# Holding six chunk loads for a last read on VectorE, and dealing the mixer's steps unevenly

## The chip, the cores and the metric

The kernel runs on one core of a Trainium2 chip. It uses TensorE (PE), VectorE (DVE), ScalarE (ACT), GpSimd (POOL), and SyncE (SP), which issues every DMA of this kernel. The metric is device time in microseconds. The kernel before took 374.99 us, the median of three runs (372.95, 374.99 and 376.47).

## The reference

Two blocks follow one another. The first is a linear attention with a decaying state, for 4 batches, 8 heads, 768 tokens and a head width of 48:

```python
for t in range(S):
    kt, vt, rt = (k[:, :, t], v[:, :, t], r[:, :, t])
    cur = np.einsum('bhd,bhe->bhde', u[None] * kt, vt)
    y[:, :, t] = np.einsum('bhd,bhde->bhe', rt, state + cur)
    state = w[None, :, :, None] * state + np.einsum('bhd,bhe->bhde', kt, vt)
```

Its heads side by side are `x` (4 x 768 x 384), which goes into the second block, a gated mixer:

```python
h = np.maximum(x @ w_in, 0.0)                 # d_ff = 1024
u, v = (h[..., :512], h[..., 512:])
v_n = (v - mean(v)) / np.sqrt(var(v) + 1e-06) # over the 512 of a token
v_s = np.einsum('ts,bsd->btd', w_spatial, v_n) + b_spatial[None, :, None]
out = (u * v_s) @ w_out
```

All of it is float32.

## The kernel before

The attention is cut into 24 chunks of 128 tokens, six to each batch. The main loop (L605) has one **period** for each chunk, numbered from 0, and one before them, -1. A period `i` goes through these parts, and each engine does its share of them in the order in which they are written; nothing is reordered.

- `g2(i)` (L362): TensorE finishes chunk `i`. It reads `r` out of the tile `rk` (L379), and then `v` out of the tile `rkv` (L389). It is 112 matmuls as the profile counts them, 88 for the first chunk of a batch.
- `fin(i)` (L391): ScalarE copies the result to `xh` (L399). Up to chunk 6 TensorE then makes the low part (`fin_low`, L412); from chunk 7 on VectorE does (L404).
- `g1(i+1)` (L312): the first half of the next chunk, 64 matmuls at L320 and L329, 48 where that chunk is the last of a batch. `g2(i)` and `g1(i+1)` are one dense stretch of small matmuls, called **zone** `i` here.
- `mid(i+1)` (L339): VectorE masks the scores (L343) and updates the state (L351 or L356, L358, L359), and ScalarE copies blocks of it (L336, L337). In the last chunk of a batch VectorE's part ends with L351.
- `load_chunk(i+3)` (L92): SP issues two DMAs, `rk` (512 KB, L98) and `rkv` (648 KB, L102). Both tiles have three buffers, so these two go into the buffers of chunk `i` and wait for the last reads of those. SP issues in order: a DMA that waits holds up all that stand behind it.
- `prep(i+2)` (L270): scaling of `rk` (L281 on GpSimd and L282 on VectorE, or L284), products on `rkv` (GpSimd, L287 to L291), a sum (L294) and the diagonal (L303).
- A few **steps** of the mixer, the larger matmuls that fill TensorE. There are 112 steps in one fixed list (L547): `moe_v` and `moe_u` with 9 matmuls each, `moe_out` with 12, `moe_sp` with 18. The number `n` at L627 says how many of the list have been done by the end of period `i`: a table for the first six periods, then an even 28 steps in six periods, and all that is left in period 23.
- In the early periods, pieces of the mixer's weights between the steps (`pour`, L581): float64 weights are turned into two float32r parts, and the spatial weights, twelve transfers `wst` (L90), are split by ScalarE (L182) and VectorE (L183). The last four of these transfers are each issued when VectorE has used up an earlier one (L261). `bulk` (L593) issues the first six and the bias after period 0, four transfers `raw` of `w_out` after period 2, and two `wst` after period 3.

So SP's order around the change is: chunk 3, six `wst` and the bias, chunk 4, chunk 5, `raw` four times, chunk 6, two `wst`, chunk 7, three `wst`, chunk 8, the last `wst`, chunk 9.

## Time and profile before

| what | us |
|---|---|
| median of three runs | 374.99 |
| the profiled execution | 374.84 |
| its span, first to last instruction | 373.1 |
| TensorE busy in matmuls | 340.5 (91%) |
| VectorE busy | 200.5 (54%) |
| GpSimd busy | 157.0 (42%) |
| ScalarE busy | 148.0 (40%) |
| DMA, share of 16 engines, queue of the kernel's own transfers | 31.2% |

The rest of the execution, 374.84 less 373.1, lies outside the span. TensorE's granted clock was 0.993 on average. A row of a timeline has the start, the time, the engine, the line and the operation, what is written and read, how many instructions were merged, and in brackets the idle time of the engine before it with what ended it; "issue" there means that the engine waited for nothing that the profile shows. Matmuls on float32 tiles count twice in the profile, since each runs as two.

### The profile page before, as it was taken

How to read it: one execution, taken by the hardware profiler on the slowest of the kernel's cores; microseconds unless marked ns; L12 is line 12 of the kernel's file. 1: busy time of each engine (PE TensorE's matmuls, PEld its weight loads, DVE VectorE, ACT ScalarE, POOL GpSimd, SP SyncE). 2: the span in 40 equal slices, each digit the busy share in tenths (PEclk: the TensorE clock that was granted, in tenths of full speed). 3: DMA queues.
4: the chain of work that ended last, by engine and by line, in shares of the span. 5: the costliest groups of instructions: out<-in, count | busy, mean ns of one | idle time of the engine just before them, and what ended most of it. 6: DMA issues, size and time to landing. Idle time of an engine off the chain costs nothing.

```text
span 373.1 us, 12304 instructions
## 1 busy us (share of the span) xinstructions
PE 340.5 (91%) x5479; PEld 310.8 (83%) x5479; DVE 200.5 (54%) x400; ACT 148.0 (40%) x325; POOL 157.0 (42%) x160
## 2 busy tenths in 40 slices
PE   2759669879999999899999989998999899999994
PEld 1427558779999998799999978898989898999994
DVE  7697855879645553664362625686451624433130
ACT  3154558584123234546131324645131336461211
POOL 5975555763554261645753444043652320013120
PEclk9999999999999999999999999999999999999998
DMA  7994755433031441333031352134041010000101
GB/s 251 413 372 135 267 204 176 170 129 105 29 124 70 131 154 52 117 132 129 2 129 65 129 186 67 72 129 131 0 152 45 2 66 4 0 0 2 56 9 63
DMA packets 14021, 41.69 MB, mean 112 GB/s; under 512 B 1680, under 2 KB 6416, under 8 KB 13968
## 3 DMA queue, kind: packets, MB, share of 16 engines
q1 hardware_dynamic: 13968, 40.90, 31.2%
q8 instruction: 43, 0.70, 0.8%
q14 instruction: 10, 0.08, 0.1%
HBM read 36.18 MB, written 4.72 MB: 110 GB/s over the span
## 4 chain that ended last, share of the span: by engine, by line
PE 82%; DVE 5%; ACT 4%; issue 4%; DMA 2%; POOL 2%; SPq 0%; ACTq 0%; DVEq 0%
PE pm L428 21%; PE pm L429 20%; PE pm L430 20%; PE xp L369 10%; PE ps L320 3%; PE ps L329 3%; DMA rkv<-rkvN 2%; ACT vs L472 1%; DVE a L343 1%; ACT ws_h L182 1%; DVE ws_l L183 1%; PE pm L498 1%; PE pm L503 1%; PE pm L499 1%; PE pm L226 1%
## 5 line engine op out<-in xcount | busy, mean ns | idle before, releaser
L516 POOL TENSOR_TENSOR g<-g,u 128x384 f32<-128x384 f32 x31 | 31.5, 1015 | 116.8 <-DVE g L515 116.7
L428 PE MATMUL pm<-ws_h,vnorm 128*128 128x384 f32 x192 | 64.9, 338 | 0.0
L430 PE MATMUL pm<-ws_h,vnorm 128*128 128x384 f32 x192 | 64.3, 335 | 0.0
L429 PE MATMUL pm<-ws_l,vnorm 128*128 128x384 f32 x192 | 64.2, 334 | 0.0
L303 POOL TENSOR_TENSOR a<-diag,dg 128x512 f32<-128x512 f32 x24 | 25.4, 1059 | 66.8 <-DVE dg L294 33.7
L182 ACT CAST gt<-g 128x384 fp32r<-128x384 f32 x32 | 16.4, 514 | 91.3 <-POOL g L516 89.3
L183 DVE TENSOR_TENSOR gt<-g,gt 128x384 fp32r<-128x384 f32 x32 | 20.9, 654 | 57.0 <-ACT gt L182 57.0
L428 PEld LDWEIGHTS pm<-ws_h,vnorm 128*128 128x128 f32 x192 | 36.0, 188 | 0.3
L429 PEld LDWEIGHTS pm<-ws_l,vnorm 128*128 128x128 f32 x192 | 36.0, 188 | 0.0
L430 PEld LDWEIGHTS pm<-ws_h,vnorm 128*128 128x128 f32 x192 | 36.0, 188 | 0.0
L428 PE MATMUL pm<-wo_h,gt 128*128 128x384 f32 x96 | 32.9, 343 | 0.0
L430 PE MATMUL pm<-wo_h,gt 128*128 128x384 f32 x96 | 32.3, 336 | 0.0
L429 PE MATMUL pm<-wo_l,gt 128*128 128x384 f32 x96 | 32.3, 336 | 0.0
L515 DVE TENSOR_TENSOR g<-pm,bb 128x384 f32<-128x384 f32 x32 | 17.7, 553 | 22.1 <-PE pm L430 22.0
L329 PE MATMUL ps<-rkv 64*64 64x48 f32 x704 | 17.8, 221 | 12.3 <-issue 8.7
L428 PE MATMUL pm<-wi_h,xh 128*128 128x512 f32 x72 | 28.7, 398 | 0.0
L430 PE MATMUL pm<-wi_h,xl 128*128 128x512 f32 x72 | 28.3, 393 | 0.1
L429 PE MATMUL pm<-wi_l,xh 128*128 128x512 f32 x72 | 28.3, 393 | 0.0
L369 PE MATMUL xp<-a,rkv 64*32 64x64 f32 x1536 | 24.1, 227 | 3.2 <-issue 3.2
L288 POOL TENSOR_TENSOR rkv<-rkv,ub 128x384 f32<-128x384 f32 x24 | 26.1, 1086 | 1.9
L449 DVE BATCH_NORM_STATS2 q<-vs 128x6 f32<-128x512 f32 x24 | 16.5, 687 | 18.6 <-ACT vs L442 18.6
L329 PEld LDWEIGHTS ps<-rkv 64*64 64x64 f32 x704 | 15.1, 139 | 13.5 <-issue 9.7
(112 smaller groups left out, 736.0 us busy)
## 6 DMA issues: line engine op xcount, KB each, us to landing
rkv<-rkvN SPq DMA_DIRECT2D x24, 648.0 KB, 5.8
rk<-rkT SPq DMA_DIRECT2D x24, 512.0 KB, 3.8
out<-ob SPq DMA_DIRECT2D x24, 192.0 KB, 1.9
raw<-w_in SPq DMA_DIRECT2D x6, 512.0 KB, 10.0
wst<-w_sp SPq DMA_DIRECT2D x12, 192.0 KB, 5.7
raw<-w_out SPq DMA_DIRECT2D x4, 384.0 KB, 8.1
bb<-b_sp SPq DMA_DIRECT2D x1, 384.0 KB, 5.6
ub<-uB SPq DMA_DIRECT2D x1, 192.0 KB, 6.6
```

The source lines that it names most:

```text
L182: nc.scalar.copy(hi, src)
L183: (eng or nc.vector).tensor_tensor(out=lo, in0=src, in1=hi.bitcast(F32), op=ALU.subtract)
L288: nc.gpsimd.tensor_tensor(out=rn, in0=rn, in1=ub, op=ALU.mult)
L303: nc.gpsimd.tensor_tensor(out=a.rearrange("s j p t -> s (j p) t"), in0=diag.unsqueeze(1).to_broadcast([P, H, HC]), in1=dg.rearrange("s j p ...
L329: nc.tensor.matmul(ps[64 * j:64 * j + 64, s0 // 64, 256 + p * D:256 + (p + 1) * D], t["kn"][s0:s0 + 64, h * D:h * D + 64], t["v"][s0:s0 + ...
L369: nc.tensor.matmul(xp[32 * g:32 * g + 32, z, jt * HC:(jt + 1) * HC], lhsT, rhs, start=(z, g) not in began, stop=True, skip_group_check=Tru ...
L428: nc.tensor.matmul(o, lh, rh, start=first, stop=False)
L429: nc.tensor.matmul(o, lh, rl, start=False, stop=False)
L430: nc.tensor.matmul(o, ll, rh, start=False, stop=last)
L449: nc.vector.bn_stats(out=q6[:, c % 3, :], in_=vs)
L515: nc.vector.tensor_tensor(out=g, in0=pm[:, 0:TH], in1=bb[:, ts_], op=ALU.add)
L516: (nc.vector if (b, t, d) == (B - 1, 1, ND - 1) else nc.gpsimd).tensor_tensor(out=g, in0=g, in1=u, op=ALU.mult)
```

## The change

After `mid(i+1)` of periods 0 to 5 VectorE gets one more instruction. It multiplies one column of chunk `i`'s `rk` by one column of its `rkv` into a tile that nobody reads. As it reads both buffers, the loads of chunk `i+3` (chunks 3 to 8) wait for it, and it stands behind the state's update on VectorE. Second, a table `ADJ` is added to `n` from period 6 on. It is not zero for nine periods, so that single steps cross the border between two periods, forwards or backwards; the order of the steps stays the same, and so does their number.

```diff
+    HOLD = 6
+    ADJ = [0, 0, 0, 0, 0, 0, 0, 0, 0, -1, 1, 0, 0, -1, 0, 1, 1, 0, -1, 1, 1, -1, 0, 0]
...
-    dmas, raws = {}, {}
+    dmas, raws, held_by = {}, {}, {}
...
             dmas[m] = [rk]
+            held_by[m] = [rk]
...
             dmas[m].append(rkv)
+            held_by[m].append(rkv)
...
+    last_read = const.tile([P, 1], F32, name="last_read")
...
             mid(i + 1)
+        if 0 <= i < HOLD:
+            rk, rkv = held_by.pop(i)
+            nc.vector.tensor_tensor(out=last_read, in0=rk[:, 0, 0, 0:1], in1=rkv[:, 0:1], op=ALU.mult)
         if i >= 0:
             load_chunk(i + 3)
         parts = prep(i + 2) if i < NM - 2 else []
-        n = 0 if i < 0 else FIRST[i] if i < NC else len(steps) if i == NM - 1 else int(10 + (i - 5) * 28 / 6)
+        n = 0 if i < 0 else FIRST[i] if i < NC else len(steps) if i == NM - 1 else int(10 + (i - 5) * 28 / 6) + ADJ[i]
```

Steps in each period, from 9 to 22, before: 4, 5, 5, 4, 5, 5, 4, 5, 5, 4, 5, 5, 4, 5. After: 3, 7, 4, 4, 4, 6, 5, 5, 4, 3, 7, 5, 2, 6.

## The prediction

> **What bounds the kernel now.** I read the page first, for the bound and for the instruction traffic.

> ```profile
> span 373.1 us, 12304 instructions
> PE 340.5 (91%) x5479; PEld 310.8 (83%) x5479; DVE 200.5 (54%) x400; ACT 148.0 (40%) x325; POOL 157.0 (42%) x160
> q8 instruction: 43, 0.70, 0.8%
> ```

> TensorE is the bound: a change that keeps its matmuls can move only its gaps, 373.1 - 340.5 = 32.6 us. The third row is a queue that carries instructions: 0.70 MB in 43 packets are 16 KB each, and 2 x 5479 instructions of TensorE over 43 are 255 a packet. So TensorE's program comes in blocks of about 256 instructions, 128 matmuls with their weight loads.

> Next, TensorE's waits: the whole span, then from 76.9 us on.

> ```profile
> PE ps L329 <- issue: 8.7, 8, 2.2
> PE xp L369 <- issue: 3.2, 1, 3.2
> ...
> PE ps L329 <- issue: 5.4, 6, 1.1
> ```

> "issue" means that nothing in the profile released it. I laid windows between the ends of such gaps and counted matmuls:

> ```profile
> 40.64:48.16 7.52, 4.35 (x127) 1.00 0.96 338
> 80.27:150.32 70.05, 68.40 (x1147) 1.00 0.30 104
> ```

> 127 and 1147 are 128 times 1 and 9, less the few semaphore instructions that aren't counted. So the gaps sit at borders of blocks: TensorE waits there for its next block. Both halves of the change bear on that. ADJ moves steps past a zone and so shifts where the borders fall in it, and the hold changes which transfers run beside a fetch.

> **ADJ: the six late gaps.** The timeline shows how many matmuls of each zone come after its gap (zones 6, 11, 16, 19, 20, 21):

> ```profile
> 80.27 0.26 PE L329 MATMUL ps<-rkv 64*64 64x48 f32 x2 [0.83 <-issue]
> 150.32 0.49 PE L329 MATMUL ps<-rkv 64*64 64x48 f32 x18 [0.96 <-issue]
> 219.44 0.37 PE L329 MATMUL ps<-rkv 64*64 64x48 f32 x6 [0.95 <-issue]
> 254.54 0.31 PE L329 MATMUL ps<-rkv 64*64 64x48 f32 x2 [1.05 <-issue]
> 273.97 0.44 PE L329 MATMUL ps<-rkv 64*64 64x48 f32 x13 [0.62 <-issue]
> 290.86 0.33 PE L329 MATMUL ps<-rkv 64*64 64x48 f32 x7 [1.01 <-issue]
> ```

> Zones have 176 matmuls, 152 in zone 6 and 160 in zone 16. Zone less rest, less 128, is the place of the border before: 22, 30, 26, 46, 35 and 41. A zone stalls, then, where a border lies early in it and the next one still inside. Where does the edge lie below which the fetch comes early enough? Counting on by 128, zones 13 to 15 have borders at 4, -8 and -1 and no gap. The stretch after the last chunk load shows the lead:

> ```profile
> 290.86:336.46 45.60, 45.60 (x493) 1.00 0.04 15
> 325.00:336.46 11.46, 11.46 (x67) 1.00 0.00 0
> 336.46:337.80 1.34, 1.34 (x10) 1.00 0.06 12
> ```

> A fetch flows at 336.46, after 493 matmuls. The border at 4 x 128 = 512 is 18 or 19 matmuls ahead, and the pace is 11.46 / 67 = 0.171 us each. So a fetch flows while TensorE is 18 short of its border; borders up to about 18 into a zone are fetched before the dense part begins. Counting what ADJ moves (9 for a `moe_v` or `moe_u`, 12 for a `moe_out`, 18 for a `moe_sp`), the borders become: zone 11 at 21 (`v13` goes before it), zone 14 at 10 (`sp110` goes behind), 16 at 14 (`o112` before), 19 at 55 (`u213` behind), 20 at 23 and 21 at 23. In zone 19 the next is at 183, outside: 1.05 us gone. Zone 16 falls under the edge: 0.95 gone; zone 14 stays free by the same edge. 21, 23 and 23 are beside zone 6's 22, which stalls 0.83; I take 0.1 us off each. Sum: **-2.3 us**. Bounds: all five gone, 0.96 + 0.95 + 1.05 + 0.62 + 1.01 = -4.6; only zone 19 helped and zone 14 newly stalled, about 0. That the short periods 18 and 21 (three and two steps) leave `mid` too little time I bound at 0 to +0.3.

> [...]

> **The hold: what it frees.** Here are the gap in zone 3, SP's queue around it, and the ends of three updates on VectorE (chunks 3, 5 and 6) with a small operation as price for the new one.

> ```profile
> 48.16 0.24 PE L369 MATMUL xp<-a,rkv 64*32 64x64 f32 x1 [3.17 <-issue]
> ...
> 37.71 0.33 SPq L98 DMA_DIRECT2D rk<-rkT  x1
> 39.60 2.03 SPq L82 DMA_DIRECT2D raw<-w_out  x4
> 48.84 0.91 SPq L90 DMA_DIRECT2D wst<-w_sp  x2
> 61.81 5.12 SPq L90 DMA_DIRECT2D wst<-w_sp  x3
> 67.04 0.37 SPq L98 DMA_DIRECT2D rk<-rkT  x1
> 67.51 0.38 SPq L102 DMA_DIRECT2D rkv<-rkvN  x1
> 71.52 0.33 SPq L90 DMA_DIRECT2D wst<-w_sp  x1
> ...
> 42.51 0.36 DVE L359 TENSOR_TENSOR s<-ps,w 128x192 f32<-128x192 f32 x1
> 59.49 0.34 DVE L351 TENSOR_TENSOR t<-s,ps 128x192 f32<-128x192 f32 x1
> 69.54 0.36 DVE L359 TENSOR_TENSOR s<-ps,w 128x192 f32<-128x192 f32 x1
> 58.37 0.17 DVE L464 TENSOR_SCALAR q<-q 128x3 f32<-128x3 f32 x1
> ```

> The gap of 3.17 us is three times a late one. Its block could be asked for from 40.64 on, when chunk 5 and four `raw` (2.7 MB) were under way. Held, chunk 5's load leaves at 42.51 + 0.36 + 0.2 = 43.1, and the fetch meets an empty queue: **-3.17**, bounds 0 and -3.17. The other early gaps at L329 (8.7 less 5.4, so 3.3 us) are of the late kind, two borders in one zone, and I leave them: the hold moves no border.

> **The hold: what it makes late.** SP issues in order, so four spatial weight transfers now queue behind later chunk loads, and ScalarE waits for them in order:

> ```profile
> 60.68 0.93 ACT L182 CAST ws_h<-wst 128x384 fp32r<-128x384 f32 x2
> 64.73 0.51 ACT L182 CAST ws_h<-wst 128x384 fp32r<-128x384 f32 x1
> 65.63 0.47 ACT L399 CAST xh<-xp 128x384 fp32r<-128x384 f32 x1
> 74.20 0.51 ACT L182 CAST ws_h<-wst 128x384 fp32r<-128x384 f32 x1 [0.51 <-DMA wst<-w_sp]
> 75.44 0.82 ACT L472 ACTIVATE vs<-vs,q 128x512 f32<-128x512 f32 x1 [0.34 <-DVE q L466]
> 66.15 0.36 PE L412 MATMUL xp<-xh,neg 128*128 128x192 f32 x1 [0.64 <-ACT xh L399]
> 75.16 0.45 PE L498 MATMUL pm<-xh,wi_h 128*128 128x384 f32 x1 [1.32 <-ACT u L504]
> ...
> DMA to landing us min/median/max: 5.8/5.8/5.8
> DMA to landing us min/median/max: 2.7/2.7/2.7
> DMA to landing us min/median/max: 5.4/5.4/5.4
> ...
> POOL a L303 <- DVE dg L294: 33.7, 10, 7.5
> ```

> (The landings are those of chunk 8's `rkv`, of the last `wst` and of the two `wst` of 48.84.) TensorE waits for ScalarE at both places, so a late `wst` there is a late TensorE. The last one first. Chunk 8's pair took 67.51 + 5.8 - 67.04 = 6.3 us, and the `wst` at 71.52 + 2.7 = 74.2 landed 0.9 after it. Held, the pair leaves at 69.54 + 0.36 + 0.2 = 70.1, lands at 76.4, and the `wst` at 77.3: 3.1 late. ScalarE has 0.34 us of slack at L472, so **+2.7 us**; bounds 0 (the `wst` overtakes) and +3.1.

> Earlier, the gain in zone 3 has to last until 65 us. Chunk 7's pair would leave at 59.49 + 0.34 + 0.2 = 60.0 in old time and land at 66.3, the next `wst` at 67.2 instead of before 64.73: +2.5, leaving -0.7 of the 3.17. The queue can be worse: it worked without a break (0.96 of the engines in 40.64 to 48.16) until the two `wst` landed at 48.84 + 0.5 + 5.4 = 54.7, and the same bytes, started 43.1 - 37.71 = 5.4 us later, end at 60.1, against their L182 at 60.68 - 3.17 = 57.5. I take the 3.17 as eaten, **0**, bounds -0.7 and +0.8 (chunk 7's pair behind that queue). The six added instructions cost 0.2 us each, on VectorE's chain once, in period 0: **+0.2**, bounds 0 and 1.2. Chunks 3 and 4 leave later too, but GpSimd, which takes them up first, idles 33.7 / 10 = 3.4 us at a time before L303, and that hides it; without this cover they would cost what they are late.

> **Sum.** 0 + 2.7 + 0.2 - 2.3 = +0.6 on the profiled execution's own 374.84 (373.1 and 1.7 outside the span, 0.15 below the median): **375.4 us**.

> **Rivals.** *Faster.* The four `wst` are not late, since their engines serve them beside the chunk loads or ScalarE's chain has slack that the rows hide. Then 374.84 - 3.17 + 0.2 - 2.3 = 369.6, and 367.3 with all five late gaps gone. For it: the ADJ places 21 to 23 are close to my edge of 18. Against: L182's 0.51 us wait on the DMA.

> *Slower: the burst only moves.* Chunk 5 and the `raw` now start as zone 3 begins and run past the next border, so the gap reappears and does not pay for chunk 7's delay: 374.84 + 2.5 + 2.7 + 0.2 = 380.2 with ADJ at 0, 377.9 with -2.3. It decides once zone 3's gap stays over 2 us and ADJ gives under 1. A second road to the 380.2 is that the gaps aren't fetches at all, so that neither half frees anything; the counts of 128 speak against it. [...]

> *Nothing happens.* The loads were late anyway, as SP waits behind `wst` (61.81, 5.12 us for three issues): ADJ alone, 372.5.

> **Chances.** Forecast, costs and gains cancel: 0.5. Faster rival 0.25, slower 0.2, nothing 0.05. Within 1% of 374.99 means 371.2 to 378.7, about what three runs spread over 372.95 to 376.47 can tell apart. So faster 0.25, same 0.55, slower 0.20. The range runs from the faster rival's 369.6 nearly to the slower one's 380.2: 369.5 to 379.5. The forecast's own goes by ADJ's bounds, 373.1 to 377.7.

> **What would show it.** Right: late gaps at zones 6, 11, 20, 21 but not 16 and 19; no 3 us gap near 48 us; ScalarE's L182 waiting over 2 us on `wst` near 60, 65 and 75 us; TensorE's first L498 after 73 us later by 2 to 3. Wrong: no DMA wait at L182, or gaps whose distances aren't multiples of 128.

## The result and the profile after

The changed kernel took 373.73 us (median of 20 runs, 371.45 to 375.25), the kernel before 375.45 (20 runs, 372.95 to 379.79). The ratio is 0.9949, with a 95% interval of 0.9927 to 0.9971: 1.9 us faster (1.1 to 2.7), which lies within 1%. An execution over 1.5% above the fastest of its kernel, such as the one of 379.79, is left out of the ratios. The prediction said 375.4, half a microsecond slower. The time is inside its range, but the sign is wrong: the kernel became a little faster.

Lines of the changed kernel are six higher than before (L182 is now L188, L329 is L335). Three rows of TensorE's waits over the whole span, and then the late gaps alone, from 77 us on:

```profile
PE ps L335 <- issue: 7.9, 6, 2.3
PE pm L504 <- ACT u L510: 1.9, 1, 1.9
PE ps L326 <- issue: 1.7, 1, 1.7
...
PE ps L335 <- issue: 3.6, 4, 1.0
```

The late gaps shrank from six with 5.4 us to four with 3.6 us. The timeline has them in zones 6, 11, 20 and 21, the four that the prediction named:

```profile
82.35 0.26 PE L335 MATMUL ps<-rkv 64*64 64x48 f32 x2 [1.02 <-issue]
154.13 0.67 PE L335 MATMUL ps<-rkv 64*64 64x48 f32 x27 [1.02 <-issue]
275.10 0.57 PE L335 MATMUL ps<-rkv 64*64 64x48 f32 x25 [0.74 <-issue]
292.70 0.57 PE L335 MATMUL ps<-rkv 64*64 64x48 f32 x24 [0.84 <-issue]
```

With 27, 25 and 24 matmuls after the gap, the borders of zones 11, 20 and 21 lie at 176 - 27 - 128 = 21, at 23 and at 24; counting the moved steps had given 21, 23 and 23. Zones 16 and 19 have no gap.

In zone 3 the 3.17 us gap is gone; all of `g2` and `g1` run through, and chunk 5's load and the four `raw` leave at 43.19 and 44.05:

```profile
45.85 0.97 PE L375 MATMUL xp<-a,rkv 64*32 64x64 f32 x64
46.75 0.70 PE L326 MATMUL ps<-rk 64*64 64x64 f32 x32
...
43.19 0.33 SPq L101 DMA_DIRECT2D rk<-rkT  x1
44.05 2.12 SPq L85 DMA_DIRECT2D raw<-w_out  x4
58.63 0.33 SPq L101 DMA_DIRECT2D rk<-rkT  x1
70.45 0.33 SPq L101 DMA_DIRECT2D rk<-rkT  x1
71.94 0.33 SPq L93 DMA_DIRECT2D wst<-w_sp  x1
```

And ScalarE waits for the spatial weights in two of the three places that the prediction gave, near 65 and 76 us but not near 60. In the second TensorE waits behind it, 1.86 us where it was 1.32. The last row is the landing of the `wst` of 71.94, 4.1 us where it was 2.7:

```profile
65.46 0.51 ACT L188 CAST ws_h<-wst 128x384 fp32r<-128x384 f32 x1 [2.19 <-DMA wst<-w_sp]
76.09 0.51 ACT L188 CAST ws_h<-wst 128x384 fp32r<-128x384 f32 x1 [1.98 <-DMA wst<-w_sp]
77.04 0.45 PE L504 MATMUL pm<-xh,wi_h 128*128 128x384 f32 x1 [1.86 <-ACT u L510]
DMA to landing us min/median/max: 4.1/4.1/4.1
```

So the steps happened, the wait near 60 us excepted. What the experiments had to settle is what each was worth.

### The profile page after: what moved, and what is told of

It reads as the page before. It is cut to its first block, busy times and chain, and to the rows that moved or that the text cites. A ratio compares the mean times of both kernels' runs of the same rounds, so it can differ in the third digit from the quotient of the medians.

```text
span 372.1 us, 12307 instructions
## 1 busy us (share of the span) xinstructions
PE 343.9 (92%) x5479; PEld 312.2 (84%) x5479; DVE 202.4 (54%) x406; ACT 148.1 (40%) x325; POOL 160.4 (43%) x160
## 4 chain that ended last, share of the span: by engine, by line
PE 82%; DMA 6%; DVE 4%; issue 3%; ACT 2%; POOL 1%; SPq 1%; DVEq 0%; ACTq 0%
PE pm L434 21%; PE pm L435 20%; PE pm L436 20%; PE xp L375 10%; PE ps L326 3%; PE ps L335 3%; DMA wst<-w_sp 2%; DMA rkv<-rkvN 2%; DMA raw<-w_out 2%; PE pm L232 1%; DVE a L349 1%; DVE ws_l L189 1%; ACT ws_h L188 1%; PE pm L504 1%; DMA out<-ob 0%
## 5 line engine op out<-in xcount | busy, mean ns | idle before, releaser
L188 ACT CAST gt<-g 128x384 fp32r<-128x384 f32 x32 | 16.4, 514 | 88.9 <-POOL g L522 86.9
L293 POOL TENSOR_TENSOR rkv<-rkv 128x384 f32<-128x384 f32 x24 | 25.2, 1049 | 7.5 <-DMA rkv<-rkvN 7.5
L335 PE MATMUL ps<-rkv 64*64 64x48 f32 x704 | 17.7, 225 | 11.4 <-issue 7.9
L294 POOL TENSOR_TENSOR rkv<-rkv,ub 128x384 f32<-128x384 f32 x24 | 27.3, 1136 | 1.9
L297 POOL TENSOR_TENSOR rkv<-rkv,tn 128x384 f32<-128x384 f32 x24 | 26.5, 1105 | 0.0
```

Of the source, the lines that this page charges most:

```text
L188: nc.scalar.copy(hi, src)
L293: (nc.vector if DV0 and m == 0 else nc.gpsimd).tensor_tensor(out=rn, in0=rn, in1=kn, op=ALU.mult)
L294: nc.gpsimd.tensor_tensor(out=rn, in0=rn, in1=ub, op=ALU.mult)
L297: (nc.vector if DV0 and m == 0 else nc.gpsimd).tensor_tensor(out=kn, in0=kn, in1=tn_f, op=ALU.mult)
L335: nc.tensor.matmul(ps[64 * j:64 * j + 64, s0 // 64, 256 + p * D:256 + (p + 1) * D], t["kn"][s0:s0 + 64, h * D:h * D + 64], t["v"][s0:s0 + ...
```

## The experiments

**Each half alone.** Theory A: the halves add, ADJ by two block gaps, the hold by zone 3's gap less the late spatial weights. Rival B: the hold makes the change faster, and ADJ does nothing.

```diff
 # hold_only
-    ADJ = [0, 0, 0, 0, 0, 0, 0, 0, 0, -1, 1, 0, 0, -1, 0, 1, 1, 0, -1, 1, 1, -1, 0, 0]
+    ADJ = [0] * 24
 # adj_only
-    HOLD = 6
+    HOLD = 0
```

> The hold alone, ADJ all zero. Theory A (the parts add: ADJ takes two block gaps, the hold frees zone 3's gap and pays for it with late spatial weights): 0 to +2 us against the kernel before, about +0.9; six block gaps after zone 6 included, as before (places 22, 30, 26, 46, 35, 41). Rival B (the hold is what makes the change faster, ADJ is worth nothing): -1 us or better.

> ADJ alone, no load held. Theory A: -2.3 to -2.9 us against the kernel before, the gaps of zones 16 and 19 gone and those of zones 6, 11, 20 and 21 there; the 3 us gap of zone 3 there again. Rival B: within 0.5 us of the kernel before.

The hold alone has a ratio of 0.9998 (0.9966 to 1.0030): -0.1 us, between -1.3 and +1.1. ADJ alone has 0.9952 (0.9915 to 0.9988): -1.8 us, between -3.2 and -0.5. A's ranges lie a little above the first and half a microsecond beyond the second, and both intervals reach into them. B wanted -1 us or better from the hold and at most 0.5 from ADJ, so as far as these intervals tell B falls: the whole gain of the change is ADJ's. The late gaps sum to 6.4 us in six for the hold alone, and 4.5 us in four for ADJ alone:

```profile
PE ps L335 <- issue: 6.4, 6, 1.4
```

```profile
PE ps L335 <- issue: 4.5, 4, 1.5
```

**Fewer held loads, with ADJ.**

```diff
 # hold_five
-    HOLD = 6
+    HOLD = 5
 # hold_chunk5
-    HOLD = 6
+    HOLD = (2,)
...
-        if 0 <= i < HOLD:
-            rk, rkv = held_by.pop(i)
+        if i in HOLD:
+            rk, rkv = held_by[i]
```

> The changed kernel with five held loads instead of six: chunk 8's load is not held, so the last transfer of spatial weights does not queue behind it. Theory A: this transfer's lateness costs TensorE 1.5 to 2.7 us, so -3.4 to -4.6 us against the kernel before, and no DMA wait over 0.6 us of ScalarE near 76 us. Rival C (ScalarE's wait there is hidden by other late work): same as the changed kernel, -1.9 us.

> The changed kernel with one held load, chunk 5's (period 2), and ADJ. Theory A: zone 3's gap of 3.2 us goes and neither of the two late spatial weights near 65 and 76 us is behind a held chunk load, so -4 to -6 us against the kernel before. Rival D (zone 3's gap does not go by chunk 5's hold alone, or it comes back in another zone): -2.3 to -2.9 us, as ADJ alone.

Five held loads: 0.9903 (0.9870 to 0.9936), -3.6 us, between -4.9 and -2.4, which is 1.7 better than six. Chunk 5's alone: 0.9883 (0.9838 to 0.9929), -4.4 us, between -6.1 and -2.7, and 2.6 better than ADJ with none; each of these two differences is uncertain by 1.5 to 2.2 us. Without chunk 8's hold ScalarE's wait for the last weights is back to its old size (it was 0.51):

```profile
ACT ws_h L188 <- DMA wst<-w_sp: 0.6, 1, 0.6
```

So the hold is a gain in one period and a loss in others, and six of them come out even. C falls. D's time touches the end of the interval, but in this kernel's profile zones 3, 4 and 5 have no gap, so D falls too.

**Held loads one at a time, without ADJ.** The three kernels below have `HOLD = (5,)`, `(4,)` and `(0, 1)` in the form above, and `ADJ = [0] * 24`.

> The kernel before with chunk 8's load alone held (period 5), no ADJ: the term that the prediction put at +2.7 us, alone. If it was sized right: +2.2 to +3.1 us, ScalarE waits 2.5 us or more for the last spatial weights near 76 us. If it was too large, as the comparison of six held loads with five says: +1.0 to +1.9 us.

> The kernel before with chunk 7's load alone held (period 4), no ADJ: the term that the prediction put at +2.5 us where nothing has been gained before it. If sized right: +2 to +2.8 us, TensorE waits near 3 us for ScalarE's xh in zone 5. If ScalarE's wait is partly hidden: 0 to +1.5 us.

> The kernel before with the loads of chunks 3 and 4 held (periods 0 and 1), no ADJ. Prediction: GpSimd's idle time hides them, +0.2 us, between 0 and 0.6. Rival: the late load of chunk 4 runs into the block fetch of zone 2 and lengthens its gap, +1 us or more.

Chunk 8 alone: 1.0025 (0.9991 to 1.0059), +0.9 us, between -0.3 and +2.2. Chunk 7 alone: 1.0056 (1.0024 to 1.0088), +2.1 us, between +0.9 and +3.3. Chunks 3 and 4: 1.0003 (0.9968 to 1.0038), +0.1 us. So chunk 7's cost was sized well; TensorE's wait for `xh` in zone 5, 0.64 us before, is 3.62 here:

```profile
71.25 0.63 PE L418 MATMUL xp<-xh,neg 128*128 128x192 f32 x2 [3.62 <-ACT xh L405]
```

The time of chunks 3 and 4 is as expected, but its interval, -1.2 to +1.4, doesn't exclude the rival's +1. In the profile the gap of zone 2 is longer (1.90 us, 1.17 before) and that of zone 3 shorter (1.31, 3.17 before), so that GpSimd's idle time hid these loads is not shown. Chunk 8's cost is under the +2.7 of the prediction, just below the +1.0 that was expected if that was too large, and ScalarE waits 2.0 us for the last weights, not 2.5. Why is seen in the changed kernel's profile, in the issue of chunk 8's `rkv` and its time to landing:

```profile
70.88 0.38 SPq L106 DMA_DIRECT2D rkv<-rkvN  x1
...
DMA to landing us min/median/max: 4.7/4.7/4.7
```

The held pair leaves at 70.45 (its `rk` is quoted above) and has landed at 70.88 + 4.7 = 75.6: 5.1 us, where the prediction took 6.3 from the pair of the kernel before. The `wst` behind it lands at 71.94 + 4.1 = 76.0, 0.5 after the pair instead of 0.9. Together they are 1.6 us quicker than the prediction had them. ScalarE's wait grew accordingly by 1.5 us (0.51 to 1.98) and not by 3.1, and TensorE's wait behind it by 0.5 (1.32 to 1.86), or by 1.0 (to 2.33) in the profile of chunk 8's hold alone. Why the transfers were quicker wasn't tested; the older pair left 0.1 us behind a `wst`, the held one 3.2 us.

**Moving every border, without touching a step.** The sharpest test of the block theory adds a few instructions to TensorE at the start, where it waits for VectorE, and leaves all steps and loads alone. The matmuls multiply zeros, and nothing reads their result.

```diff
         pt = ps_m.tile([P, 512], F32, name="pm")
+        for _ in range(14 if p == 0 else 0):
+            nc.tensor.matmul(pt[0:64, 256:320], zz, zz, start=True, stop=True, skip_group_check=True)
         nc.tensor.transpose(pt[:, 0:P], tt[:, p, :], eye)
```

> The kernel before with 14 small matmuls on zeros (56 instructions of TensorE, matmuls and weight loads) at its start, where TensorE waits for VectorE anyway; no step is moved, no load is held. Theory A (the gaps are waits for blocks of 256 instructions; a zone stalls where a border lies about 19 to 48 matmuls into it): every border moves 28 matmuls towards the start of its zone, so the gaps of zones 6, 11, 16, 19, 20 and 21 (5.4 us of idle time) go and one comes in zone 17: -4 to -6 us, more than ADJ brings. Rival E (ADJ helps by how steps and chunks are mixed, not by where borders fall): 0 to +1 us, as work is only added.

> The same with 64 small matmuls, 256 instructions: a whole block, so that every border lies where it lay before. Theory A: all eight gaps at the same places, -0.8 to +1 us against the kernel before. Rival F (the added matmuls help by themselves, by warming TensorE's clock early): as much as the shift by 56 or more.

56 instructions: 0.9782 (0.9741 to 0.9823), **-8.2 us**, from 14 useless matmuls. From 77 us on the profile has one gap in a zone, in zone 17 (and one of 1.2 in a mixer step):

```profile
PE pm L436 <- issue: 1.2, 1, 1.2
PE ps L337 <- issue: 1.0, 1, 1.0
```

It is more than A said, because zone 3's gap went too (0.2 us of 3.17 are left), without any hold. The likely reason is that with no gap in zone 2 the next block is asked for earlier; this was not tested. In the profiled executions zone 7 begins 3.5 us earlier than in the kernel before (84.39, not 87.90), and 3.6 us more are saved behind that. An earlier start of TensorE by itself is no rival: zone 0 begins at 15.39 us, not 15.80, so it explains 0.4 us at most.

256 instructions, the whole block: 1.0104 (1.0074 to 1.0135), +3.9 us, more than the +1 that A allowed, with all six late gaps at the places where they were:

```profile
PE ps L337 <- issue: 6.2, 6, 1.2
...
1.05 10.32 PE L162 MATMUL pm<-tmp 128*64 128x64 f32 x128 [1.05 <-DVE tmp L128]
```

The 64 matmuls ran until 11.4 us at a slow start (128 records in 10.32 us, 0.081 each, where the 32 of L328 at 11.89 us take 0.69, 0.022 each) and made zone 0 begin 1.8 us later. The granted clock is a likely part of the rest, which was not tested: it was 0.974 to 0.984 in the ten runs of this kernel, and 0.981 to 0.995 in the 15 of the kernel before beside them. The added matmuls don't help by themselves, so F falls, and so does E: it is the place of the borders that counts.

**Putting parts together.** Two kernels with chunk 5's load held, and one without a hold:

```diff
 # best_a: HOLD = (2,), ADJ as in the change, range(4 if p == 0 else 0)
 # best_b: HOLD = (2,), ADJ = [0] * 24, range(14 if p == 0 else 0)
 # best_c: HOLD = 0, range(14 if p == 0 else 0), and
+    ADJ = [0, 0, 0, 0, 0, 0, 0, 0, 0, 0, 0, 0, 0, 0, 0, 0, -1, 0, 0, 0, 0, 0, 0, 0]
```

> ADJ, chunk 5's load alone held, and 4 small matmuls (16 instructions) at the start, which move ADJ's borders at 21, 23, 23 and 22 to 13 to 15, under the edge. Theory A: no gap after zone 3 but perhaps small ones, 4 us less than with chunk 5's hold and ADJ alone: -7 to -9 us against the kernel before. If the edge lies lower than 13, -4 to -5 us.

> No ADJ, chunk 5's load alone held, and 14 small matmuls (56 instructions). Theory A: gaps of blocks in zone 17 alone, zone 3's gap gone by the hold: -7 to -9 us against the kernel before, which would make ADJ needless.

> No load held, 14 small matmuls (56 instructions) at the start, and one step later in period 16 (ADJ of -1 there, nowhere else), which moves zone 17's border from 46 to 55, so that its next one falls outside the zone. Theory A: no block gap left after zone 3, 1 to 1.4 us less than with the 56 instructions alone: -9 to -10 us against the kernel before. If gaps and time part company: as with the 56 instructions alone, -8.2 us.

`best_a`: 0.9842 (0.9799 to 0.9885), -5.9 us; `best_b`: 0.9860 (0.9813 to 0.9907), -5.3 us. Both gain less than was expected. In `best_a` the gaps of zones 6, 11, 20 and 21 are gone, so borders at 13 to 15 are harmless. But zone 0's gap is 3.26 us (2.16 before), zone 19 got one of 0.83, as its border moved from 55 to 47 and the next one back inside, and a fetch came late in a mixer step after zone 4. In `best_b` one came late in zone 4 itself, with the transfers at 0.95 of the DMA engines in the gap (51.18 to 53.84 us). The first row is of `best_a`, the second of `best_b`:

```profile
57.92 0.50 PE L437 MATMUL pm<-wi_l,xh 128*128 128x512 f32 x1 [2.65 <-issue]
...
53.84 0.26 PE L328 MATMUL ps<-rk 64*64 64x64 f32 x1 [2.66 <-issue]
```

So the hold and the shift don't add. The likely reason is that once the borders lie well, the hold only moves a burst of transfers to where it hurts. `best_c` has no hold and no gap in any zone after zone 0; 0.9722 (0.9680 to 0.9763), **-10.5 us**, the best of all, and faster than both kernels. Its waits of TensorE from 76 us on:

```profile
PE xp L420 <- ACT xh L407: 2.1, 1, 2.1
PE pm L436 <- issue: 1.1, 1, 1.1
```

## Why the prediction was right and wrong

*The gaps are waits for blocks of 256 instructions: right.* The distances, the places after ADJ, and the shift by 56 and by 256 all say so. In the trace of the kernel before, 127 matmuls, 127 weight loads and 2 semaphore instructions start from 40.64 us on and before 48.16, together 256, and 1147, 1147 and 10 from 80.27 on and before 150.32, together 9 times 256. From zone 6 on, no zone with a border at up to 18 matmuls stalls in these profiles (in zone 19 the shift by 56 makes 46 - 28 = 18), and those with one at 21 to 47 and the next still inside do, so the edge of about 18 held. What the waits cost is plain: nine gaps of the kernel before take 8.7 + 3.2 = 11.9 us of TensorE's time.

*ADJ, -2.3: right, within its interval.* Measured -1.8 (-3.2 to -0.5). Zones 16 and 19 lost their gaps, zones 11, 20 and 21 kept theirs, zone 14 got none. The profiles say it more sharply: from the start of zone 7 to the end the four kernels with ADJ and no added matmuls take 282.4 to 283.2 us, and the kernel before, the hold alone, chunk 7's hold and the hold of chunks 3 and 4 take 284.7 to 285.8, 2.3 more in the mean. That this is the predicted number to a tenth is partly luck: the 0.1 us off each of zones 11, 20 and 21 didn't come (1.02, 0.74 and 0.84 against 0.96, 0.62 and 1.01), and what came in its place wasn't followed up.

*Zone 3's gap, -3.17: right.* In the six profiles with chunk 5's load held it is gone or down to 0.4 us at most. From the start of zone 3 to that of zone 5 the four of them without added matmuls take 16.6 to 16.9 us, the kernel before 19.4. Chunk 5's hold by itself was worth 2.6 us beside ADJ.

*The step that failed is the sum of the hold, 0 + 2.7 + 0.2 = +2.9.* Measured, it is -0.1 (-1.3 to +1.1) alone, and 0.9949 against 0.9952 beside ADJ. The mechanism was right, and so were two of the three places; the term of chunk 8's pair, +2.7, was too large. It measured +0.9 alone, and 1.7 between six holds and five. Its working took 6.3 us for the pair and 0.9 for the `wst` behind it; they measured 5.1 and 0.5, so the weights came 1.6 us earlier than it had them. The second term, 0 for zone 3's gain less chunk 7's delay, was nearly right: -2.6 and +2.1 give -0.5. With +0.1 for chunks 3 and 4 and +0.9 to +1.7 for chunk 8 the parts sum to +0.5 to +1.3. The parts are each uncertain by 1 to 2 us, so that their sum can't be told from -0.1; chunk 6's hold wasn't run alone, and how the rest divides stays open. With the hold at 0, the prediction's own sum would have read 374.84 - 2.3 = 372.5, its fourth case, whose reason (the loads were late anyway) was not the true one.

*The places where the prediction asked to be shown wrong:* no 3 us gap near 48 us, yes; L182 waiting over 2 us near 60, 65 and 75, yes at 65 (2.19) and nearly at 76 (1.98), no at 60; the first L498 after 73 us later by 2 to 3, 77.04 instead of 75.16, so 1.9. The new gap of 1.69 us in zone 5, where a fetch (a 16 KB packet of q8 at 62.99 us) runs beside chunk 7's held load (its `rkv` from 59.1 to 63.9), was not foreseen. It took the place of the wait for ScalarE's `xh`, which is 2.95 us in the profile of the hold alone, where this gap is missing, and nothing in the changed kernel.

## What to carry to other kernels

Where TensorE's waits say "issue" in the middle of a run of small matmuls, count the instructions between them: if the distances are multiples of one number, here 128 matmuls with their weight loads, they are likely fetches, and a few harmless instructions in an idle place at the start can be worth more than a new order of the work, here 8.2 us against 1.8. Try such a shift before tuning an order by time alone, since an edit that adds or moves instructions of TensorE also shifts borders behind it (ADJ took zone 11's from 30 to 21). And a load that is made to wait moves what stands behind it in its queue (with chunk 5's load at 43.19 us instead of 37.71, the four `raw` left at 44.05 instead of 39.60): list who waits for those, and hold only the load that pays.

## What the runs showed of the hardware that was not expected

A gap on TensorE can cost a second time. In the changed kernel, the stretch from 38.23 to 41.64 us holds zone 2's gap and is busy 1.09 of 3.41 us; in the next 3.41 us the granted clock is half, and again after the one that holds zone 5's gap:

```profile
38.23:41.64 3.41, 1.09 (x27) 0.99 0.02 5
41.64:45.05 3.41, 3.41 (x7) 0.50 0.18 54
45.05:48.47 3.42, 3.42 (x181) 1.00 1.00 403
61.95:65.36 3.41, 1.72 (x111) 1.00 0.67 256
65.53:68.94 3.41, 3.41 (x64) 0.50 0.23 62
```

The columns are the stretch, TensorE's length and busy time with its count, the granted clock, the DMA share and the rate. Six matmuls that split spatial weights fall into the second row. Here they are in the timeline after, and then before (L250):

```profile
41.31 3.80 PE L256 MATMUL pm<-wst,eye 128*128 128x384 f32 x6
```

```profile
41.21 2.12 PE L250 MATMUL pm<-wst,eye 128*128 128x384 f32 x6
```

```profile
43.46:46.87 3.41, 1.53 (x111) 1.00 1.00 397
46.87:50.28 3.41, 2.12 (x70) 1.00 0.77 254
```

So, by these counts, it is worth about 1.7 us (3.80 less 2.12) whether a gap falls into one such stretch or is cut by two, and that looks like chance: before the end of its span the kernel before had one stretch at half clock in its profiled run, the changed one three, and `best_c` none. This is a likely reason why single runs of one kernel lie up to 7 us apart. In the 27 runs of the kernel before that were made beside the hold alone, the seven with a mean granted clock of 0.981 or less took 378.2 to 379.9 us, the other twenty 373.1 to 377.1; what sets the clock of a run was not tested.
